# Attention, a top-2 mixture and a top-1 mixture on one core: where the softmax sums, the one-hot products and the first lo parts are computed

## The chip, the core and the metric

The program runs on one NeuronCore of a Trainium2 chip. The metric is the time in device microseconds (us) of one execution. TensorE multiplies matrices into PSUM, VectorE and ScalarE do elementwise work, GpSimd does elementwise work and issues the indirect DMAs, and SyncE issues most other DMAs. In the profile they are PE, DVE, ACT, POOL and SP.

## The reference, cut to what matters

Three stages follow each other. All arithmetic is float32.

```python
# attention: q, k, v are [4, 8, 576, 64]
scores = scale * q @ k^T, masked to blocks of 64: block_i >= block_j
attn = exp(scores - max); attn = attn / (sum(attn) + 1e-9)
x = (attn @ v) as [2304, 512]
# first mixture: 8 experts, the best 2 of each row
noisy = x @ w_gate + log1p(exp(x @ w_noise)) * noise
weights = softmax over the two best; out = sum of weight * (relu(x @ w1[e]) @ w2[e])
# second mixture, on the first one's output: 8 experts, the best 1 of each row
logits = x @ w_gate2 + bias[modality]; e = argmax
out = softmax(logits)[e] * (relu(x @ w1[e]) @ w2[e])
```

## The kernel before

**Precision.** Products that need float32 are made from pairs of a reduced type: a tensor is copied into a hi part by ScalarE, and a lo part, the tensor less its hi part, is computed by another engine. Three matrix products (hi by hi, hi by lo, lo by hi) then stand for one. For a tile of weights this is `Stage.split` (line 450): `act.activation` makes `hi` (in the profile `wh`), `eng.tensor_sub` makes `lo` (`wl`), 128 x 1024 elements at a time. The caller chooses `eng`.

**Attention** goes in 16 pairs of heads (`pair(p)`, line 849), each cut into named steps: scores `S`, maxima `M` (VectorE), exponentials `E` (ScalarE, which also sum up into `ss`), transposes `B` with hi and lo copies `H` and `L` (`PTh`, `PTl`), products with the values `V`, projections `X`, copies `XC`. `R` (line 971) adds the two sums of the last block, `R1` (974) adds 1e-9 to nine sums, `R2` (977) takes reciprocals into `rr`; all three run on VectorE. On GpSimd, `VS` splits the values (`vs`) and `out_rows` (1067) scales a pair's rows by `rr` into `x` and its logits into `LH`.

**The order** of the attention stage is made by a planner at build time (lines 1201 to 1348). Every step has a due time (`SCHED`, line 19, plus 14.5 us per pair) and a list of steps before it (`before`). `clk` holds a modelled time for each engine, from cost formulas (lines 80 to 99). At each turn the planner emits the step of TensorE, ScalarE or VectorE that can start first, among equals the one due first. GpSimd's work is put out along with other steps. What the planner emits is the fixed order of each engine's queue.

**The first routing** (`route`, line 643) is a chain of small VectorE operations on up to 10 columns of 128 rows: logits `lg`, two one-hot choices `oh` (by `onehot`), a mask `m`, counts on TensorE, positions, then for each batch of 576 rows `hot_b` (`sl_ob`, 128 x 1280), `hot_a` (`sl_oa`, 128 x 400, and the product `sl_ov`, 128 x 2000) and `lists`, ten matrix products of the two. It runs for two batches after pair 7, one after pair 11 and one after pair 15 (`route_at`, line 1294); its steps are slipped in between the attention steps. The first two of these calls (`slow` true, three products in all) compute `sl_ov` on GpSimd, and `made` (line 282) tells `lists` when the planner takes it to be done; the last call computes it on VectorE. The last one ends with `ids1`, the rows of every expert (`last_route`, line 1122).

**The jobs** of the mixtures are passes of one expert over a set of rows: `mm1` (first layer, evicted into `kp` or `hh` by ScalarE and `kp` or `hl` by VectorE), then `mm2` (second layer). Job `j00` starts early: its four first-layer weight tiles are loaded into `xs` (called `pre`) and split on GpSimd at planned times (line 1305), and its steps `JT` to `JV` with the splits `JS0` to `JS3` (line 1178: `JS0` and `JS1` on GpSimd, `JS2` and `JS3` on VectorE, tiles `kld` and `qld` of 512 columns each) end the attention stage. The other jobs go through `run` (line 1366): for the first mixture with `ea` and `eb` as `[gps]` (line 1531), so GpSimd makes every lo part, and for the second with VectorE, or VectorE and GpSimd in turn. SyncE loads up to four tiles of weights ahead into `raw`; a buffer is free when its hi and lo parts are made. GpSimd also issues the gathers of rows (`xr`), the scatters of results (`X`) and of logits (`LG`).

## Time and profile before

| | us |
|---|---|
| median of 3 runs (lowest, highest) | 1046.46 (1046.31, 1047.7) |
| the profiled execution, its own time | 1041.64 |
| span of the profiled execution | 1039.6 |
| busy: TensorE matmul, VectorE, ScalarE, GpSimd | 987.5, 741.4, 518.9, 534.2 |
| chain that ended last, share of the span | PE 49%, issue 4%, POOL 3%, DVE 2% |

The profiled execution is one execution; its time is its span and some 2 us around it. Attention takes about the first 300 us, the first mixture runs to about 760, the second to the end. All helpers record line 71, so instructions are told apart by the tiles they write and read (`out<-in`).

### The profile page before, as it was taken

To read this page: it belongs to the slowest core of one execution; us is meant where nothing else is said; L and a number is where in the kernel's file an instruction comes from. 1 tells how busy PE (TensorE), PEld (TensorE's weight loads), DVE (VectorE), ACT (ScalarE), POOL (GpSimd) and SP (SyncE) were. 2 spreads that over 40 slices of the span, in tenths; PEclk is the share of its full clock that TensorE was granted. 3 is DMA by queue.
4 is the path that set the end of the run, shared out by engine and by line. 5 is a ranking of instruction groups with operands and counts; after the bars stand their busy time and mean duration, and the time that the engine had idled before them with its cause. 6 is when DMAs were issued, how large, how long until landed. Compare 5 with 4: busy or idle time off the path is not lost.

```text
span 1039.6 us, 17514 instructions
## 1 busy us (share of the span) xinstructions
PE 987.5 (95%) x6090; PEld 879.0 (85%) x6090; DVE 741.4 (71%) x1766; ACT 518.9 (50%) x1156; POOL 534.2 (51%) x420
## 2 busy tenths in 40 slices
PE   7999998997998799999999999999999999999996
PEld 6888887776787789898989899898978888999995
DVE  6778779888868689647768493948798885554551
ACT  5887876766654225333333333333324545555651
POOL 6123142272346558977668584847658345333231
PEclk8999998998999899999999999999999999999999
DMA  5465433321117455655545372735167767677630
GB/s 127 110 189 163 147 97 96 89 60 39 54 55 212 163 122 132 182 144 134 111 125 120 104 142 81 158 87 102 16 179 204 259 187 253 217 224 225 205 103 13
DMA packets 155954, 141.08 MB, mean 136 GB/s; under 512 B 73929, under 2 KB 122441, under 8 KB 155730
## 3 DMA queue, kind: packets, MB, share of 16 engines
q1 hardware_dynamic: 137794, 106.65, 34.2%
q0 software_dynamic: 18064, 33.23, 15.8%
q8 instruction: 51, 0.84, 0.3%
q14 instruction: 45, 0.37, 0.1%
HBM read 112.01 MB, written 28.36 MB: 135 GB/s over the span
## 4 chain that ended last, share of the span: by engine, by line
PE 49%; issue 4%; POOL 3%; DVE 2%; DMA 1%; ACT 0%; POOLq 0%; SPq 0%
PE ph L71 25%; PE py L71 22%; PE px L71 2%; POOL wl L71 2%; DMA xr<-X,ids 1%; DVE wl L71 1%; POOL LG L71 0%; DMA raw<-in_moe_w_dram 0%; POOL X L71 0%; DMA lgx<-LG 0%; PE pt L71 0%; DVE g_l L71 0%; POOL out_dram L71 0%; DVE g_t L71 0%; DVE kp L71 0%
## 5 line engine op out<-in xcount | busy, mean ns | idle before, releaser
L71 POOL TENSOR_TENSOR wl<-raw,wh 128x1024 fp32r<-128x1024 f32 x88 | 226.8, 2618 | 120.0 <-ACT wh L71 108.1
L71 PE MATMUL ph<-xth,wh 128*128 128x320 f32 (+2 forms) x800 | 242.1, 303 | 6.5 <-DVE kp L71 6.5
L71 PE MATMUL ph<-xtl,wh 128*128 128x320 f32 (+2 forms) x800 | 240.7, 301 | 0.0
L71 PE MATMUL ph<-xth,wl 128*128 128x320 f32 (+2 forms) x800 | 240.6, 301 | 0.0
L71 DVE SCALAR_TENSOR_TENSOR zero<-py,gts,wgb 128x512 f32<-128x512 f32 x304 | 227.5, 748 | 8.2
L71 PE MATMUL py<-wh,kp 128*128 128x512 f32 x496 | 167.9, 399 | 0.0
L71 PEld LDWEIGHTS ph<-xth,wh 128*128 128x128 f32 x800 | 152.4, 190 | 8.2 <-DVE kp L71 7.5
L71 PEld LDWEIGHTS ph<-xtl,wh 128*128 128x128 f32 x800 | 152.5, 191 | 0.7
L71 PEld LDWEIGHTS ph<-xth,wl 128*128 128x128 f32 x800 | 152.4, 190 | 0.0
L71 ACT ACTIVATE wh<-raw 128x1024 fp32r<-128x1024 f32 x144 | 150.9, 1053 | 0.6 <-DMA raw<-in_moe_w_dram 0.4
L71 ACT ACTIVATE yr<-py,gts 128x512 f32<-128x512 f32 x60 | 41.4, 690 | 147.7 <-PE py L71 104.9
L71 PEld LDWEIGHTS py<-wh,kp 128*128 128x128 f32 x496 | 93.9, 189 | 18.7
L71 DVE SCALAR_TENSOR_TENSOR hl<-ph,hh 128x320 fp32r<-128x320 f32 (+2 forms) x100 | 46.4, 466 | 76.3 <-ACT hh L71 76.3
L71 PE MATMUL ps<-kh,kp 128*128 128x256 f32 (+5 forms) x320 | 98.4, 349 | 2.2 <-ACT kp L71 1.0
L71 PE MATMUL py<-wl,kp 128*128 128x512 f32 x248 | 97.2, 392 | 0.0
L71 PE MATMUL py<-wh,hh 128*128 128x512 f32 x232 | 93.9, 405 | 0.0
L71 DVE TENSOR_TENSOR xtl<-px,xth 128x512 fp32r<-128x512 f32 x58 | 40.0, 690 | 74.3 <-ACT xth L71 68.2
L71 PE MATMUL py<-wl,hh 128*128 128x512 f32 x232 | 90.6, 390 | 1.3 <-POOL wl L71 1.3
L71 PE MATMUL py<-wh,hl 128*128 128x512 f32 x232 | 90.8, 391 | 0.0
L71 ACT ACTIVATE p<-ps,nm 128x288 f32<-128x288 f32 (+8 forms) x160 | 79.1, 500 | 22.4 <-DVE nm L71 20.8
L71 DVE TENSOR_TENSOR wl<-raw,wh 128x1024 fp32r<-128x1024 f32 x56 | 70.0, 1259 | 27.8 <-ACT wh L71 27.4
L71 ACT ACTIVATE hh<-ph 128x320 fp32r<-128x320 f32 (+2 forms) x100 | 41.9, 419 | 94.4 <-PE ph L71 91.2
(250 smaller groups left out, 1886.5 us busy)
## 6 DMA issues: line engine op xcount, KB each, us to landing
raw<-in_moe_w_dram SPq DMA_DIRECT2D x144, 512.0 KB
X<-zero SPq DMA_DIRECT2D x13, 512.0 KB
kld<-in_k_dram SPq DMA_DIRECT2D x32, 128.0 KB
qld<-in_q_dram SPq DMA_DIRECT2D x32, 128.0 KB
vld<-in_v_dram SPq DMA_DIRECT2D x32, 128.0 KB
X<-x SPq DMA_DIRECT2D x16, 256.0 KB
xs<-in_moe_w_dram SPq DMA_DIRECT2D x4, 512.0 KB
wgb<-WG2T POOLq DMA_DIRECT2D x1, 2048.0 KB
```

The costliest lines, as they stand in the source:

```text
L71: return f(*a, **kw)
```

## The change

The two sums `R` and `R1` become one step `R` on GpSimd, emitted as soon as a pair's last exponential is. `hot_a` computes its product on VectorE always, in two pieces where it is large; the parameter `slow` and `made` go. The splits of `xs`, of `JS0` and `JS1`, and those of `run` that are emitted before `ids1` use VectorE; the pieces from `xs` are cut to 512 columns.

```diff
--- before.py
+++ after.py
@@ -279,21 +279,22 @@
             yield 1.6
             return ob
 
-        made = [0]
-
-        def hot_a(pool, a, n, a0, na, vals, eng):
+        def hot_a(pool, a, n, a0, na, vals):
 
             oa = pool.tile([128, n, na], BF16, name="sl_oa")
             ov = pool.tile([128, n, NV, na], BF16, name="sl_ov")
             vec.tensor_tensor(oa, bc(lane[:, None, a0:a0 + na], [128, n, na]), bc(a[:, :, None], [128, n, na]), op=OP.is_equal)
             yield .8
-            eng.tensor_tensor(ov, bc(oa[:, :, None, :], [128, n, NV, na]), bc(vals[:, :, :, None], [128, n, NV, na]), op=OP.mult)
-            made[0] = clk["pool"] if eng is gps else 0
-            yield .3
+            m = -(-n // 2) if n * na > 200 else n
+            for c in range(0, n, m):
+                s = slice(c, min(c + m, n))
+                vec.tensor_tensor(ov[:, s], bc(oa[:, s, None, :], [128, s.stop - c, NV, na]),
+                                  bc(vals[:, s, :, None], [128, s.stop - c, NV, na]), op=OP.mult)
+                yield .3
             return ov
 
         def lists(pl, ob, ov, n, first=True, last=True):
-            yield "pe", made[0]
+            yield "pe", 0
             for i in range(n):
                 ten.matmul(pl.rearrange("p v a -> p (v a)"), ob[:, i], ov[:, i].rearrange("p v a -> p (v a)"),
                                  start=(first and i == 0), stop=(last and i == n - 1))
@@ -455,7 +456,11 @@
                 m = 1024 // len(parts)
                 for x, raw in enumerate(parts):
                     act.activation(hi[:, m * x:m * x + m], raw, AF.Copy)
-                    eng.tensor_sub(lo[:, m * x:m * x + m], raw, hi[:, m * x:m * x + m].bitcast(F32))
+
+                    k = 512 if parts[0] is pre else m
+                    for c in range(0, m, k):
+                        d = slice(m * x + c, m * x + c + k)
+                        eng.tensor_sub(lo[:, d], raw[:, c:c + k], hi[:, d].bitcast(F32))
                 (j.wa if w == "a" else j.wb).append([t.rearrange("p (n c) -> p n c", n=4 if w == "a" else 2) for t in (hi, lo)])
 
         class Job:
@@ -640,7 +645,7 @@
         stage = Stage([j00, j10] + firsts + seconds)
 
 
-        def route(b0, nb, slow):
+        def route(b0, nb):
 
             C = 5 * nb
             bs = slice(5 * b0, 5 * (b0 + nb))
@@ -743,7 +748,7 @@
             for b in range(nb):
                 n = slice(10 * b, 10 * b + 10)
                 ob = yield from hot_b(rt, bl[:, n], 10)
-                ov = yield from hot_a(rt, a[:, n], 10, 0, NA1, va[:, n], gps if slow else vec)
+                ov = yield from hot_a(rt, a[:, n], 10, 0, NA1, va[:, n])
                 yield from lists(pl, ob, ov, 10, b == 0, b == nb - 1)
             if b0 == 0:
                 vec.tensor_copy(acc1, pl)
@@ -969,10 +974,8 @@
                         ex(st["s", 8][a], 288 * a, 8, 8 + a)
 
                 def R():
-                    vec.tensor_add(st["ss"][:, 8:9], st["ss"][:, 8:9], st["ss"][:, 9:10])
-
-                def R1():
-                    vec.tensor_scalar(st["ss"][:, 0:9], st["ss"][:, 0:9], 1e-9, None, op0=OP.add)
+                    gps.tensor_add(st["ss"][:, 8:9], st["ss"][:, 8:9], st["ss"][:, 9:10])
+                    gps.tensor_scalar(st["ss"][:, 0:9], st["ss"][:, 0:9], 1e-9, None, op0=OP.add)
 
                 def R2():
                     ss = st["ss"]
@@ -985,7 +988,7 @@
                     two(i)
                 for i in range(4, 8):
                     one(i)
-                f.update(S8=S8, M8=M8, N8=N8, E8=E8, R=R, R1=R1, R2=R2)
+                f.update(S8=S8, M8=M8, N8=N8, E8=E8, R=R, R2=R2)
 
 
                 blocks = [(n, i, j) for j, n0 in ((0, 0), (1, 9), (2, 16), (3, 22)) for n, i in enumerate(range(2 * j, 9), n0)]
@@ -1120,7 +1123,7 @@
                     flags.add("early")
 
             def last_route():
-                yield from route(B - 1, 1, False)
+                yield from route(B - 1, 1)
                 yield from slot_ids(rt, acc1, NA1, 64, pad1.rearrange("p e t -> p (e t)"), ids1, gts1)
                 flags.add("ids1")
                 for t in range(j11.nt):
@@ -1129,7 +1132,7 @@
 
             def routes(i):
                 if i < 2:
-                    yield from route((B - 2) * i, B - 2 - i, True)
+                    yield from route((B - 2) * i, B - 2 - i)
                     yield from early(i)
                 else:
                     yield from last_route()
@@ -1176,7 +1179,7 @@
                     hid_(m)
 
                 def S_(i):
-                    stage.split(vec if i in (2, 3) else gps)
+                    stage.split(vec)
                     fetch_b(1)
                 for i in range(NQ):
                     f["JS%d" % i] = lambda i=i: S_(i)
@@ -1199,23 +1202,25 @@
 
 
             TT, OFF = SCHED[0], dict(SCHED[1])
-            OFF.update(N8=OFF["M8"] + .1, R1=OFF["R"] + .1, R2=OFF["R"] + .2)
+            OFF.update(N8=OFF["M8"] + .1, R2=OFF.pop("R"))
             kinds = dict(T="pe", M="pe", H="act", R="act", S="act", L="dve", V="dve")
 
             def engine(n):
+                if n in ("R", "VS"):
+                    return "pool"
                 if n[0] == "J":
                     return kinds[n[1]]
                 if n[0] in "TSBV" or n in ("X0", "X1"):
                     return "pe"
                 return "act" if n[0] in "HCE" or n in ("QH", "KH", "A4", "XC0", "XC1") else "dve"
 
-            lag = {"pe": .26, "act": .15, "dve": .13}
+            lag = {"pe": .26, "act": .15, "dve": .13, "pool": .3}
             blk = (0, 2, 4, 5, 6, 7, 8)
             S_, E_ = ["S%d" % i for i in blk], ["E%d" % i for i in blk]
             B_, L_ = ["B%d" % m for m in range(6)] + ["BT"], ["L%d" % m for m in range(6)] + ["LT"]
             before = {"TQ": [], "TK": [], "T4": ["TK"], "QH": ["TQ"], "QL": ["QH"], "KH": ["TK"], "KL": ["KH"], "A4": ["T4"], "D4": ["A4"],
-                      "R": E_, "BT": ["E8"], "HT": ["BT"], "LT": ["HT"], "VX": ["L0", "VS"], "CX": ["VX"], "V0": L_ + ["VS"], "V1": L_ + ["VS"],
-                      "C0": ["V0", "CX"], "C1": ["V1", "CX"], "X0": ["C0"], "X1": ["C1"], "XC0": ["X0", "R2"], "XC1": ["X1", "R2"], "R1": ["R"], "R2": ["R1"]}
+                      "BT": ["E8"], "HT": ["BT"], "LT": ["HT"], "VX": ["L0", "VS"], "CX": ["VX"], "V0": L_ + ["VS"], "V1": L_ + ["VS"],
+                      "C0": ["V0", "CX"], "C1": ["V1", "CX"], "X0": ["C0"], "X1": ["C1"], "XC0": ["X0", "R2"], "XC1": ["X1", "R2"], "R2": ["R"]}
             for i in blk:
                 before.update({"S%d" % i: ["QL", "KL"] + ["D4"] * (i == 8), "M%d" % i: ["S%d" % i], "E%d" % i: ["M%d" % i]})
             before.update({"N8": ["M8"], "E8": ["N8"]})
@@ -1257,7 +1262,9 @@
                     steps[p] = pair(p) if p < NPAIR else first_steps()
                 clk["base"] = t
                 steps[p][n]()
-                fin[p, n] = clk["pool" if n == "VS" else engine(n)]
+                fin[p, n] = clk[engine(n)]
+                if n in E_ and all((p, x) in fin for x in E_):
+                    emit(p, "R", t)
                 if n in ("V0", "V1", "VX") and all((p, x) in fin for x in ("V0", "V1", "VX")) and p + 2 < NPAIR:
                     emit(p + 2, "VS", t)
                 if n == "VS" and p + 2 < NPAIR:
@@ -1278,7 +1285,7 @@
                     if p >= k:
                         if (p - k, d) not in fin:
                             return None
-                        t = max(t, fin[p - k, d] + (.3 if d == "VS" else 0 if d[0] in "FG" else lag[engine(d)]))
+                        t = max(t, fin[p - k, d] + (0 if d[0] in "FG" else lag[engine(d)]))
                 if n[0] in bank and e == "pe":
                     b = bank[n[0]][0]
                     m = 2 if n == "S8" else 1
@@ -1302,7 +1309,7 @@
                 at(60 + 10 * i, lambda a=a: blank(*a))
             for i in range(NQ):
                 at(110 + 14 * i, lambda: stage.fetch(1))
-                at(110 + 14 * i + 11, lambda: stage.split(gps))
+                at(110 + 14 * i + 11, lambda: stage.split(vec))
             while any(todo.values()) or len(aside) > 1 or "early" not in flags:
                 best = None
                 for e, l in todo.items():
@@ -1377,7 +1384,7 @@
                 for f in range(len(j.hh), NF // 128):
                     j.mm1(f, hp_)
                     if f in fs and len(j.wb) < NQ:
-                        stage.split(eb[fs.index(f) % len(eb)])
+                        stage.split(eb[fs.index(f) % len(eb)] if "ids1" in flags else vec)
                     stage.fetch(ah)
                     rows()
                     filler()
@@ -1399,7 +1406,7 @@
                                 if left[2]:
                                     break
                                 until(nx.need[0])
-                            stage.split(ea[left[1] % len(ea)])
+                            stage.split(ea[left[1] % len(ea)] if "ids1" in flags else vec)
                             left[1] += 1
                     stage.fetch(ah)
                     filler()
@@ -1517,7 +1524,7 @@
                 for i in range(2):
                     n = slice(HN * i, HN * i + HN)
                     ob = yield from hot_b(pool, bl[:, n], HN)
-                    ov = yield from hot_a(pool, a[:, n], HN, a0, na, vals2[:, n], vec)
+                    ov = yield from hot_a(pool, a[:, n], HN, a0, na, vals2[:, n])
                     yield from lists(pl, ob, ov, HN, i == 0, i == 1)
                 acc = pool.tile([128, NV, na], F32, name="g_acc")
                 vec.tensor_copy(acc, pl)
@@ -1563,7 +1570,7 @@
                 for i in range(B):
                     n = slice(10 * i, 10 * i + 10)
                     ob = done(hot_b(r1, bl[:, n], 10))
-                    ov = done(hot_a(r1, a[:, n], 10, 0, NT2, vals.rearrange("p c k v -> p (c k) v")[:, n], vec))
+                    ov = done(hot_a(r1, a[:, n], 10, 0, NT2, vals.rearrange("p c k v -> p (c k) v")[:, n]))
                     done(lists(pl, ob, ov, 10, i == 0, i == B - 1))
                 acc = r1.tile([128, NV, NT2], F32, name="acco")
                 vec.tensor_copy(acc, pl)
```

## Rows read from the trace of the kernel before

**Rows 1.** Stages: length, busy PE, PEld, DVE, ACT, POOL, granted clock, DMA.
```profile
20.00:150.00 130.00, 128.40 (x860) 112.51 (x860) 101.54 (x250) 103.25 (x329) 29.92 (x46) 0.99 0.52 142
...
150.00:300.00 150.00, 133.36 (x876) 113.96 (x876) 127.09 (x333) 101.76 (x311) 56.14 (x57) 0.95 0.24 65
...
300.00:362.00 62.00, 52.73 (x303) 47.27 (x303) 44.90 (x86) 23.17 (x44) 38.07 (x29) 0.92 0.53 159
...
442.00:760.00 318.00, 318.00 (x1865) 291.55 (x1864) 220.43 (x573) 115.77 (x191) 214.84 (x121) 1.00 0.49 112
```

**Rows 2.** Timeline of TensorE, the five long gaps: start, length; in brackets idle before, releaser.
```profile
173.03 2.82 PE L71 MATMUL pt<-ident,p 128*128 128x128 f32 x12 [4.16 <-DVE PTl L71]
...
238.46 1.12 PE L71 MATMUL pt<-ident,p 128*128 128x128 f32 x4 [5.47 <-DVE PTl L71]
...
274.00 0.63 PE L71 MATMUL pt<-ident,p 128*128 128x128 f32 x4 [2.58 <-DVE oh L71]
...
326.83 0.18 PE L71 MATMUL pt<-m,tri 128*128 128x40 bf16 x1 [3.79 <-DVE m L71]
...
342.94 0.69 PE L71 MATMUL ph<-xth,wh 128*128 128x384 f32 x1 [3.96 <-DVE kp L71]
```

**Rows 3.** Stretches of half clock behind four gaps, and around 274; columns as rows 1.
```profile
173.00:177.80 4.80, 4.77 (x23) 4.68 (x24) 4.80 (x15) 2.65 (x8) 0.00 (x0) 0.51 0.26 90
...
238.50:242.60 4.10, 4.10 (x20) 4.10 (x21) 2.92 (x7) 2.16 (x6) 0.00 (x0) 0.50 0.02 4
...
327.90:331.30 3.40, 3.40 (x12) 2.81 (x10) 1.95 (x5) 1.75 (x3) 0.99 (x1) 0.50 0.46 151
...
343.00:348.40 5.40, 5.40 (x17) 5.40 (x18) 5.24 (x10) 1.15 (x2) 0.00 (x0) 0.50 0.33 98
...
260.00:280.00 20.00, 17.42 (x119) 15.16 (x118) 17.76 (x52) 14.62 (x49) 6.29 (x8) 1.00 0.23 69
```

**Rows 4.** Timeline of VectorE: stretched instructions.
```profile
166.99 1.40 DVE L71 TENSOR_SCALAR ss<-ss 128x9 f32<-128x9 f32 x1
...
168.30 2.87 DVE L71 TENSOR_TENSOR ex<-ex,u 128x80 f32<-128x80 f32 x1
...
231.67 4.96 DVE L71 TENSOR_SCALAR ss<-ss 128x9 f32<-128x9 f32 x1
...
319.63 2.32 DVE L71 TENSOR_TENSOR oh<-oh,e_rev 128x40 f32<-128x40 f32 x1
...
324.61 2.17 DVE L71 TENSOR_TENSOR m<-oh 128x40 bf16<-128x40 f32 x1
...
334.54 7.89 DVE L71 TENSOR_SCALAR d<-e 128x5 f32<-128x5 f32 x1
```

**Rows 5.** Timeline of GpSimd at three of these places.
```profile
168.73 2.34 POOL L71 TENSOR_TENSOR wl<-xs,wh 128x1024 fp32r<-128x1024 f32 x1
...
233.06 3.53 POOL L71 TENSOR_TENSOR sl_ov<-sl_oa,vals 128x2000 bf16<-128x2000 bf16 x1
...
334.80 7.60 POOL L71 TENSOR_TENSOR wl<-raw,wh 128x1024 fp32r<-128x1024 f32 x3
```

**Rows 6.** Groups of VectorE, 150 to 300 us: busy us, mean ns.
```profile
L71 DVE TENSOR_SCALAR ss<-ss 128x9 f32<-128x9 f32 x8 | 13.2, 1648 | 0.9 <-ACT p L71 0.9
...
L71 DVE TENSOR_TENSOR ss<-ss 128x1 f32<-128x1 f32 x7 | 1.1, 156 | 0.2 <-ACT p L71 0.2
```

**Rows 7.** Groups of GpSimd, 0 to 362 us.
```profile
L71 POOL TENSOR_TENSOR wl<-raw,wh 128x1024 fp32r<-128x1024 f32 x8 | 19.6, 2604 | 16.0 <-ACT wh L71 16.0
...
L71 POOL TENSOR_SCALAR mn<-midf 128x18 f32<-128x18 f32 x1 | 0.2, 218 | 0.1
```

**Rows 8.** Groups of VectorE, 300 to 362 us; the last line from the whole profile.
```profile
L71 DVE TENSOR_TENSOR sl_ov<-sl_oa,vals 128x2000 bf16<-128x2000 bf16 x1 | 2.2, 2236 | 0.0
...
L71 DVE TENSOR_TENSOR wl<-kld,wh 128x512 fp32r<-128x512 f32 x2 | 1.4, 681 | 0.0
...
L71 DVE TENSOR_TENSOR wl<-raw,wh 128x1024 fp32r<-128x1024 f32 x56 | 70.0, 1259 | 27.8 <-ACT wh L71 27.4
```

## The prediction

> **What bounds the kernel now.** I read the stages first, then TensorE's gaps, then what VectorE and GpSimd did in them. By stage [rows 1], TensorE works 318.00 of 318 us from 442 to 760, so whatever is won earlier is carried straight through that stage. From 20 to 150 it works 128.40 of 130. The loss lies between: 150 to 300 holds 133.36 us of work in 150, and 300 to 362 holds 52.73 in 62. The timeline of TensorE puts 20.0 us of that into five gaps [rows 2]: 4.16, 5.47, 2.58, 3.79 and 3.96 us. Each ends on a VectorE instruction. Four of them cost twice: the granted clock stands at about 0.5 (1.2 of 2.4 GHz) when TensorE comes back [rows 3], and the 4.77, 4.10, 3.40 and 5.40 us that it then works would have taken half, so 2.4 + 2.05 + 1.7 + 2.7 = 8.8 us are lost. The 2.58 us gap at 274 left the clock at 1.00 (last of rows 3).
>
> Why is VectorE late? Look at durations, not order [rows 4]. `ss`, a sum over 9 columns, takes 1.40 and 4.96 us; `ex`, 80 columns, 2.87; `oh` and `m`, 40 columns, 2.32 and 2.17; `d`, 5 columns, 7.89. Lay GpSimd beside them [rows 5]: its lo part of weights ends at 168.73 + 2.34 = 171.07 and `ex` at 171.17; its one-hot product at 233.06 + 3.53 = 236.59 and `ss` at 236.63; its three lo parts at 334.80 + 7.60 = 342.40 and `d` at 342.43. VectorE stands until GpSimd's last instruction in a row is through; it does not get in between two of them. This is the price that the change goes after.
>
> The Trainium skill (SBUF — State Buffer, Who interferes with whom) gives a reason: a VectorE instruction with two SBUF inputs, or in a mode using both ports, and a GpSimd instruction that reads SBUF exclude each other, and the later one waits in full. The endings above agree.
>
> **The parts and their prices.**
>
> *Sums on GpSimd.* Sixteen pairs lose two VectorE instructions each. Between 150 and 300 the eight adds of 1e-9 take 13.2 us; seven adds of one column take 0.156 each [rows 6]. At that price eight would take 1.3, so 11.9 us of standing go. On GpSimd the two ops cost some 0.2 us each (its 18-column op takes 0.2 [rows 7]), 0.4 per pair. They wait there for the last exponential, and the next pair's values and the scaled rows queue behind them; `R2` waits for them on VectorE. The cover is the schedule: `R2` is due at +9.0 us, the last exponential at -1.75 us, ten us of slack. I charge nothing; if the cover went, `R2` and all VectorE work behind it would be late by at most one GpSimd run, some 3.5 us as the product above. Between 20 and 150 at most 1.6 us can be won [rows 1]; I take 0.
>
> *The lo parts of the first jobs.* Four from `xs` go to VectorE in halves: a 512-column piece there takes 0.681 us [rows 8], so 1.4 each, 5.4 in all. Two of the four in the first job's steps (`JS0`, `JS1`) follow, 2.7 us, in a stretch where TensorE has no gap: nothing. Eight from `raw` before `ids1` [rows 7] at 1.259 each [rows 8] are 10.1 us. No DMA is added; a raw buffer is freed after 1.26 instead of 2.6 us, so SyncE's loads can only start earlier.
>
> *The one-hot products.* Three go from GpSimd (3.53 us) to VectorE, 2.236 us whole [rows 8]; cut in two it pays a second start, 0.10 us by two pieces of 0.681 against one of 1.259, so 2.3 each, 7.0 in all. The fourth was there already and is only cut. `lists` on TensorE no longer waits for GpSimd.
>
> So VectorE gets 5.4 + 2.7 + 10.1 + 7.0 = 25.2 us of new work. What counts is each gap:
> - 173 us: `ss` and `ex` give back 1.24 + 2.7; the lo part adds 1.4. Gain 2.5, and 2.4 of clock, since a gap of 1.7 is left, shorter than the harmless 2.58.
> - 238 us: `ss` gives back 4.8, the product costs 2.3. Gain 2.5, gap left 3.0. This lies between the 2.58 after which the clock held and the 3.79 after which it fell, nearer to the first: I book the 2.05.
> - 274 us: GpSimd's own work (values, scaled rows) stays and still holds the routing's operations; only the share of `ss` goes, about 11.9 / 8 = 1.5.
> - 327 us: `oh` and `m` give back 4.2 (each over the 0.156 of one column), two lo parts add 2.5. Gain 1.7, and 1.7 of clock.
> - 343 us: `d` gives back 7.7, three lo parts add 3.8. That would close the gap; but VectorE is then nearly full there (eight evictions, six lo parts and the last routing within the second job's first layer), so I take 3.0 of the 3.96, and 2.7 of clock.
>
> Sum: 2.5 + 2.4 + 2.5 + 2.05 + 1.5 + 1.7 + 1.7 + 3.0 + 2.7 = 20.0 us.
>
> Against it stands one unknown: the fourteen new pieces between 150 and 300 (eight from `xs`, six of products) also read two SBUF tiles. No row shows such a piece held. Below: 0, if they fall between GpSimd's runs. Above: held as `ss` is, 1.5 each, 21 us. GpSimd's work there falls from 56.14 us [rows 1] by 4 x 2.34 and 3 x 3.53 to 36 of 150, 24%; 14 x 0.24 x 1.5 = 5 us, of which I put 3 on the path. **Sum: 17 us.** The profiled execution took 1041.6 us (span 1039.6 and 2.0 around it), 4.8 under the median of the runs, 1046.5. I take the difference off the median: **1029.5 us**.
>
> **The rivals.**
>
> *The standing only changes its victim.* If every second one of the fourteen pieces is held like `ss`, that is 7 x 1.5 = 10.5 us, and the 2.5 + 2.4 + 2.5 + 2.05 + 1.5 = 11 us won between 150 and 300 are gone. Only the stretch after 300, where little but DMA issues stays on GpSimd, gives its 1.7 + 1.7 + 3.0 + 2.7 = 9.1: about 1037.5 us. (With all fourteen held, 21 us, nothing is won at all.) For it: the pieces meet the same GpSimd work as `ss`. Against: they lie elsewhere than `ss`, which is emitted just as GpSimd scales a pair's rows, and they are short. The Trainium skill (SBUF — State Buffer, Who interferes with whom) speaks for it: an instruction with two SBUF inputs waits in full if GpSimd came first. By that rule each of the fourteen that comes second stands; the trace agrees for `ex`, which reads two SBUF tiles.
>
> *VectorE becomes the bound (slower).* It is busy 127.09 of 150 and 44.90 of 62 us [rows 1], standing included. Its queue is in order: a lo part ahead of an eviction holds the PSUM bank that TensorE needs next. If all 25.2 us of new work reach TensorE, five gaps of 20.0 us become 25.2, and the clock falls as before: 1046.5 + 5 = 1051.5 us. It decides from the point where TensorE's waits for VectorE between 150 and 362 exceed 20 us. Against it: 11.9 us of `ss`, 2.7 of `ex`, 4.2 and 7.7 after 300, 26 us of standing, leave the same queue.
>
> *All gaps close.* The five gaps and the clock: 20.0 + 8.8 = 28.8, 1017.7 us. Against: the gap at 274 is made by work that stays.
>
> *A new order eats it.* The planner builds another order of the attention steps from the changed costs, and the second routing's gates are placed by the same clock. The gain moves a few us either way, or is lost: 1046 us.
>
> **How the numbers follow.** Forecast 0.60 (own range 1022 to 1037), standing moved 0.16, all gaps close 0.10, slower 0.09, lost in the order 0.05. The range 1018 to 1043 leaves out the slower case, the lost one and the tip of the full one. A difference of 0.2% (2 us) is about what a measurement of this kernel can tell from none. Faster: 0.60 + 0.15 + 0.10 = 0.85; slower 0.10; the same 0.05.
>
> **What would show it.** `ss` gone from VectorE; none of its small operations over 2 us between 150 and 360; lo parts of 0.68 and 1.26 us on VectorE there; TensorE's gaps before its solid stage under 10 us in sum; at most one stretch at 0.5 of the clock after 150; the solid stage beginning some 17 us earlier and as long as before. I am wrong if gaps as large end on VectorE's lo parts or products, if these pieces last far longer than 0.7 to 1.3 us, or if the stage after 760 grows by what was won.

## The result, and the profile after

The changed kernel takes **1028.93 us** (median of 4 runs, 1028.7 to 1030.77) against 1046.38 us for the kernel before (4 runs beside it, 1044.7 to 1047.7): a ratio of **0.9838, 95% interval 0.982 to 0.9856**. The forecast was 1029.5 us. Its profiled execution took 1028.72 us with a span of 1026.9, close to its median; that of before took 1041.64, which is 4.8 us under its median. So the two traces can account for 12.7 us of span, not for 17.4. The kernel before and the changed one were measured beside each other a second time, at the end of the experiments: there the gain was 10.6 us (1041.09 to 1030.49), and the two intervals do not meet. So the gain is known only as 10.6 to 17.4 us.

The page of the changed kernel, part 1 and two groups of part 5: VectorE is busy 17 us less than before although it got new work, GpSimd 36 us less.

```profile
PE 983.7 (96%) x6090; PEld 875.1 (85%) x6090; DVE 724.0 (71%) x1761; ACT 519.3 (51%) x1156; POOL 498.4 (49%) x433
...
L71 POOL TENSOR_TENSOR wl<-raw,wh 128x1024 fp32r<-128x1024 f32 x80 | 207.5, 2623 | 105.3 <-ACT wh L71 91.1
...
L71 DVE TENSOR_TENSOR wl<-raw,wh 128x1024 fp32r<-128x1024 f32 x64 | 79.6, 1252 | 29.7 <-ACT wh L71 29.5
```

Eight lo parts from `raw` have moved: 64 on VectorE where [rows 8] has 56.

Stages of the changed kernel (length, then busy PE, PEld, DVE, ACT, POOL, granted clock, DMA share, GB/s); the last three lines are the stretches of half clock between 150 and 427:

```profile
150.00:300.00 150.00, 138.74 (x922) 118.30 (x922) 130.28 (x347) 103.82 (x316) 45.64 (x67) 0.98 0.28 73
300.00:346.00 46.00, 41.59 (x248) 36.72 (x247) 34.44 (x85) 20.57 (x37) 8.01 (x12) 1.00 0.61 175
...
427.00:746.00 319.00, 319.00 (x1874) 292.74 (x1873) 221.52 (x575) 115.47 (x192) 215.66 (x121) 1.00 0.50 111
...
170.60:174.00 3.40, 3.17 (x15) 3.18 (x16) 3.40 (x13) 1.91 (x6) 0.00 (x0) 0.50 0.81 206
...
211.50:214.90 3.40, 3.40 (x17) 3.31 (x16) 3.40 (x6) 2.75 (x8) 0.00 (x0) 0.50 0.40 112
...
382.20:385.60 3.40, 3.06 (x7) 2.48 (x8) 0.28 (x2) 0.00 (x0) 3.40 (x2) 0.50 0.98 272
```

Against [rows 1], 150 to 300 holds 922 matmuls where it held 876, and its clock is 0.98 for 0.95. The next stretch has its clock at 1.00 (0.92 before). The solid stage is as solid as it was, and as long.

Two milestones place the gain, and serve all the experiments. **A** is the start of the last `ps<-kh,wh`, a product of the first job's steps; there are 32 of them in each kernel, and they end the attention stage. **B** is TensorE's return from the wait for the gathered rows `xr`. A came at 314.1 us before and comes at 307.2: 6.9 us won. B came at 361.3 and comes at 346.0: 15.3 us, 8.4 of them between A and B. The first layer of a later job (the first `ph` of 320 columns) starts at 425.43 (438.28 before): 12.85 us, so 2.5 were given back. Here and in the table below, differences are taken between rounded times.

The timeline of TensorE in the changed kernel (start, length; in brackets the idle time before and who ended it):

```profile
170.82 1.97 PE L71 MATMUL pt<-ident,p 128*128 128x128 f32 x8 [2.23 <-DVE PTl L71]
...
190.45 0.66 PE L71 MATMUL pt<-ident,p 128*128 128x128 f32 x4 [1.26 <-DVE PTl L71]
...
210.63 0.66 PE L71 MATMUL pt<-ident,p 128*128 128x128 f32 x4 [3.33 <-DVE PTl L71]
...
249.39 0.77 PE L71 MATMUL pt<-ident,p 128*128 128x128 f32 x5 [1.16 <-DVE PTl L71]
...
267.07 0.63 PE L71 MATMUL pt<-ident,p 128*128 128x128 f32 x4 [0.56 <-DVE pos L71]
...
319.15 0.18 PE L71 MATMUL pt<-m,tri 128*128 128x40 bf16 x1 [1.09 <-DVE m L71]
...
332.43 0.45 PE L71 MATMUL ph<-xth,wh 128*128 128x384 f32 x1 [0.39 <-DVE kp L71]
...
346.00 0.66 PE L71 MATMUL px<-ident,xr 128*128 128x128 f32 x4 [2.87 <-DMA xr<-X,ids]
...
382.54 0.80 PE L71 MATMUL py<-wh,kp 128*128 128x512 f32 x1 [3.86 <-DVE zero L71]
```

Of the five gaps of [rows 2], 20.0 us in sum, the first is 2.23 us now. The 5.47 us stood at the second batch's product of the first routing; in the changed kernel that product runs at 228 to 232 us, and no gap of 0.5 us or more lies between 219 and 249. Where the second routing begins, 1.16 and 0.56 stand for 2.58, and after A 1.09 and 0.39 for 3.79 and 3.96. A gap of 3.33 at 210 is new. Two waits took some back: `xr` now costs 2.87 us (1.45 before), and a bank held by `zero`, the product of the logits on VectorE, costs 3.86 us at 382, which before did not cost anything.

VectorE at 150 to 300 in the changed kernel, timeline:

```profile
150.10 1.71 DVE L71 TENSOR_TENSOR wl<-xs,wh 128x512 fp32r<-128x512 f32 x2 [2.03 <-ACT wh L71]
...
167.24 2.25 DVE L71 TENSOR_TENSOR wl<-xs,wh 128x512 fp32r<-128x512 f32 x2 [0.57 <-ACT wh L71]
...
186.25 3.43 DVE L71 TENSOR_TENSOR wl<-xs,wh 128x512 fp32r<-128x512 f32 x2 [1.65 <-ACT wh L71]
...
205.03 1.71 DVE L71 TENSOR_TENSOR wl<-xs,wh 128x512 fp32r<-128x512 f32 x2 [1.02 <-ACT wh L71]
206.67 3.12 DVE L71 TENSOR_TENSOR g<-e,g 128x10 f32<-128x10 f32 x1
```

Its groups there (busy us, mean ns, idle before):

```profile
L71 DVE TENSOR_TENSOR wl<-xs,wh 128x512 fp32r<-128x512 f32 x8 | 9.1, 1178 | 5.3 <-ACT wh L71 5.3
...
L71 DVE TENSOR_TENSOR sl_ov<-sl_oa,vals 128x1000 bf16<-128x1000 bf16 x6 | 7.1, 1186 | 0.0
```

And GpSimd beside `g`, timeline:

```profile
206.86 1.68 POOL L71 TENSOR_TENSOR vs<-vld,vs 128x512 fp32r<-128x512 f32 x2
208.51 1.25 POOL L71 TENSOR_TENSOR x<-xu,rr 128x640 f32<-128x640 f32 x1
209.73 0.45 POOL L71 TENSOR_TENSOR LH<-xu,rr 128x160 f32<-128x160 f32 x1
```

This reads as [rows 4, 5] did, with one difference. The lo pieces are held (9.1 us for eight, where 0.681 each would be 5.4), and `g`, 10 columns, stands 3.12 us until GpSimd's `x` ends at 208.51 + 1.25 = 209.76; `g` ends at 209.79. But GpSimd's row goes on with `LH` at 209.73, and `g` did not wait for it: "it does not get in between two of them" holds for the rows that the prediction read, not for every row. What is new is 5.3 us in four waits in which VectorE stood with a lo part from `xs` at the head of its queue and ScalarE's hi part not yet made. The gap of 3.33 us at 210 follows directly on such a wait, two lo pieces and `g`.

### The profile page after: what moved, and what is told of

Read it like the earlier page. It is cut to its first block, busy times and chain, and to the rows that moved or that the text cites. A ratio compares the mean times of both kernels' runs of the same rounds, so it can differ in the third digit from the quotient of the medians.

```text
span 1026.9 us, 17498 instructions
## 1 busy us (share of the span) xinstructions
PE 983.7 (96%) x6090; PEld 875.1 (85%) x6090; DVE 724.0 (71%) x1761; ACT 519.3 (51%) x1156; POOL 498.4 (49%) x433
## 4 chain that ended last, share of the span: by engine, by line
PE 78%; DVE 9%; issue 5%; ACT 3%; POOL 2%; DMA 2%; POOLq 0%; SPq 0%; ACTq 0%
PE ph L71 27%; PE py L71 25%; PE pt L71 9%; PE ps L71 7%; PE pa L71 6%; PE px L71 2%; DVE wl L71 2%; DMA xr<-X,ids 1%; POOL wl L71 1%; DVE PTl L71 1%; ACT p L71 1%; ACT wh L71 1%; DVE nm L71 1%; DVE kp L71 1%; POOL LG L71 0%
## 5 line engine op out<-in xcount | busy, mean ns | idle before, releaser
L71 POOL TENSOR_TENSOR wl<-raw,wh 128x1024 fp32r<-128x1024 f32 x80 | 207.5, 2623 | 105.3 <-ACT wh L71 91.1
L71 DVE SCALAR_TENSOR_TENSOR zero<-py,gts,wgb 128x512 f32<-128x512 f32 x296 | 221.6, 749 | 8.2
L71 PEld LDWEIGHTS py<-wh,kp 128*128 128x128 f32 x496 | 93.9, 189 | 22.7 <-DVE zero L71 4.1
L71 DVE TENSOR_TENSOR wl<-raw,wh 128x1024 fp32r<-128x1024 f32 x64 | 79.6, 1252 | 29.7 <-ACT wh L71 29.5
L71 POOL DMA_INDIRECT xr<-X,ids x55 | 57.8, 1051 | 75.2 <-PE px L71 45.1
```

The costliest lines, as they stand in the source:

```text
L71: return f(*a, **kw)
```

## The experiments

Each run has the kernel before beside it on the same chip. Its median there was 1043.46 us (27 runs) for engines alone, order alone, sums back and lo parts back, 1043.28 (14) for the run without the add, products back, the logits read from SBUF and the first run of later lo parts, and 1041.09 (11) for the other four. Ratios are to these. The medians of before differ by up to 5 us from series to series, so runs of different series are compared by their ratios; those of the changed kernel are 0.9838 (0.982 to 0.9856) and 0.9906 (0.9887 to 0.9925). The theory after the result: VectorE instructions of some forms (two SBUF inputs, or a `TENSOR_SCALAR` on SBUF) stand while GpSimd runs; the change takes those holds away, and that is the gain. The rival: the planner made a better order, and the engines matter little.

### Engines or order

**Engines alone.** The planner is charged as before and emits the order of before; only the engine of the instructions changes.

```diff
+    vec_p, gps_v = Timed(nc.vector, "pool", pool_cost), Timed(nc.gpsimd, "dve", dve_cost)
-                    vec.tensor_scalar(st["ss"][:, 0:9], st["ss"][:, 0:9], 1e-9, None, op0=OP.add)
+                    gps_v.tensor_scalar(st["ss"][:, 0:9], st["ss"][:, 0:9], 1e-9, None, op0=OP.add)
-                at(110 + 14 * i + 11, lambda: stage.split(gps))
+                at(110 + 14 * i + 11, lambda: stage.split(vec_p))
```

(not shown: the other moved instructions, likewise; products and lo parts stay in one piece, as before)

> The kernel before, whose planner is charged as before, so that every queue of TensorE, ScalarE and VectorE keeps its order; only the engine of the sums, of the first lo parts and of the three products is the changed one. Theory (GpSimd's runs hold VectorE up): the five gaps shrink although the order is the old one, 1031 to 1037 us. Rival (the planner's new order makes the gain): 1044 to 1049 us.

Measured: 1051.61 us, ratio **1.0087 (1.0059 to 1.0115)**, slower. The theory as it stood falls, and the rival's range is passed too. Its stage, its waits of VectorE and of TensorE from 150 to 305 us (sum in us, number, longest), then the last of these waits in the kernel before, and VectorE's timeline at one of them:

```profile
150.00:300.00 150.00, 125.68 (x788) 108.03 (x788) 114.91 (x296) 94.81 (x288) 42.64 (x62) 0.91 0.23 63
```

```profile
DVE wl L71 <- ACT wh L71: 6.9, 4, 2.4
...
DVE rr L71 <- POOL ss L71: 5.4, 3, 2.7
...
PE pt L71 <- DVE PTl L71: 22.7, 8, 4.5
```

```profile
PE pt L71 <- DVE PTl L71: 13.4, 6, 5.5
```

```profile
149.96 1.23 DVE L71 TENSOR_TENSOR wl<-xs,wh 128x1024 fp32r<-128x1024 f32 x1 [2.02 <-ACT wh L71]
153.90 0.75 DVE L71 RECIPROCAL rr<-ss 64x5 f32<-64x5 f32 x4 [2.71 <-POOL ss L71]
```

In six microseconds VectorE stands 2.02 us for a hi part and 2.71 us for GpSimd's sum, and the evictions `PTl` that TensorE needs are queued behind both. Where `ss` had been held for GpSimd, `rr` now waits for GpSimd. The holds of `ss` are gone, waits in order took their place, and other holds stay (`sl_ov` takes 3.53 us at 245.20, 2.236 alone [rows 8]): A comes at 327.3 us, 13.2 later than before. After A, where only lo parts and the last routing are concerned, the same kernel gains: from A to B it needs 39.8 us, before 47.2, the changed kernel 38.8.

**Order alone.** The reverse: the order of the change, the engines of before (not shown: the products and the lo parts of the jobs, likewise).

```diff
+    vec_p, gps_v = Timed(nc.vector, "pool", pool_cost), Timed(nc.gpsimd, "dve", dve_cost)
-                    gps.tensor_scalar(st["ss"][:, 0:9], st["ss"][:, 0:9], 1e-9, None, op0=OP.add)
+                    vec_p.tensor_scalar(st["ss"][:, 0:9], st["ss"][:, 0:9], 1e-9, None, op0=OP.add)
-                at(110 + 14 * i + 11, lambda: stage.split(vec))
+                at(110 + 14 * i + 11, lambda: stage.split(gps_v))
```

> The changed kernel's order, with the sums, the first lo parts and the three products back on the engines that they had before. Theory (holds): VectorE is held up again by lo parts and products, 1042 to 1052 us, small VectorE operations of 2 us and more again. Rival (order): 1027 to 1032 us.

Measured: 1040.74 us, 0.998 (0.9956 to 1.0003): no change that can be told. Timelines of TensorE, VectorE and GpSimd in it:

```profile
171.57 1.97 PE L71 MATMUL pt<-ident,p 128*128 128x128 f32 x8 [3.88 <-DVE PTl L71]
...
321.00 0.66 PE L71 MATMUL px<-ident,xs 128*128 128x128 f32 x4 [3.52 <-DVE xtl L71]
...
339.53 0.69 PE L71 MATMUL ph<-xth,wh 128*128 128x384 f32 x1 [4.97 <-DVE kp L71]
```

```profile
329.35 6.60 DVE L71 TENSOR_SCALAR sl_a<-sl_a 128x10 f32<-128x10 f32 x1
```

```profile
328.29 7.62 POOL L71 TENSOR_TENSOR wl<-raw,wh 128x1024 fp32r<-128x1024 f32 x3
```

The holds after A are back, as `sl_a` for 6.60 us until three lo parts on GpSimd are through (329.35 + 6.60 = 335.95, 328.29 + 7.62 = 335.91): from A to B 49.1 us. But A comes at 307.8, 6.3 us earlier than before, nearly all that the changed kernel has. Of that 1.2 was there before the first gap began (171.57 - 3.88 = 167.69, before 168.87, changed 168.59). The adds of 1e-9 are still on VectorE, only elsewhere: seven of them between 150 and 300 have a mean of 601 ns, where [rows 6] has 1648. So both fall in part: up to A the new order by itself gives most of what the change has, from A to B only the engine gives anything.

**Engines alone, sums given to GpSimd at once.** If it is the late sum that `rr` waits for, giving it out as soon as the last exponential is emitted, as the change does, should help (not shown: the two sums are in `RS`; `R` and `R1` only charge their planned time).

```diff
                 fin[p, n] = clk["pool" if n == "VS" else engine(n)]
+                if n in E_ and all((p, x) in fin for x in E_):
+                    steps[p]["RS"]()
```

> The engines-only kernel (old order of TensorE, ScalarE and VectorE, changed engines) with one difference: GpSimd gets the sums as soon as a pair's last exponential is emitted, as in the changed kernel, and not at the old place of the steps. Theory (the loss of the engines-only kernel is 5.4 us of VectorE waiting for sums that stood behind values on GpSimd, and lo parts put in without slack): 1042 to 1047 us, VectorE's wait for the sums mostly gone. Rival (it is the lo parts and products alone): 1049 to 1053 us.

Measured: 1054.88 us, 1.0125 (1.01 to 1.015). The theory was wrong. VectorE's wait for the sums there, beside the same 6.9 us for hi parts:

```profile
DVE rr L71 <- POOL ss L974: 4.9, 3, 2.7
```

The wait of `rr` is 4.9 us instead of 5.4: on GpSimd the sum still stands behind the split of the values `vs`. What the change has and this kernel lacks is a place for `R2` that is computed from GpSimd's modelled time, later in VectorE's queue; in the changed kernel no wait of VectorE for `ss` appears, and `rr` starts 2 to 10 us behind its sum. Which of the unplanned pieces (`R2`, lo parts, products) costs most of the 8 to 14 us was not separated.

### What each part gives

The first of these runs keeps the order of before. In the others the planner charges the engine that is used and makes an order of its own, so engine and order change together.

**Only the held instruction taken away.** Before, in its own order, without the add of 1e-9, whose time the planner still charges.

```diff
-                    vec.tensor_scalar(st["ss"][:, 0:9], st["ss"][:, 0:9], 1e-9, None, op0=OP.add)
+                    clk["dve"] = max(clk["dve"], clk["base"]) + dve_cost("tensor_scalar", st["ss"][:, 0:9], None, {})
```

> The kernel before without the add of 1e-9 to the sums (left out; the sums are 1 or more), the planner charged as if it were there, so that the order of all queues is the old one. It takes 16 VectorE instructions away and adds nothing. Theory (standing of ss is on the path): 11.9 us of standing between 150 and 300 go, the gaps at 173, 238 and 274 us shrink by 1.2, 4.8 and 1.5 and one half-clock stretch goes: 6 to 10 us under the kernel before. Rival (the next two-input operation in VectorE's queue is held in its place): within 2 us of the kernel before.

Measured: 1035.16 us, **0.9909 (0.988 to 0.9938)**, 8.1 us less, within the expected 6 to 10. TensorE's timeline where [rows 2] has 5.47 us, and the stage:

```profile
230.00 0.66 PE L71 MATMUL pt<-ident,p 128*128 128x128 f32 x4 [0.59 <-DVE PTl L71]
```

```profile
150.00:300.00 150.00, 141.04 (x958) 121.77 (x957) 119.80 (x335) 105.03 (x320) 61.41 (x59) 0.98 0.26 70
```

A comes 12.0 us earlier, at 302.1; from A to B it is 47.6 us, as before. The 12.0 are too much: this execution took 1029.43 us, the fastest of the five, and it was 2.2 us ahead before the gap at 173 began. By the medians sixteen adds on nine columns give 8 us, in the order of before. By its columns such an instruction is worth a fraction of a microsecond; its price is the hold [rows 6].

**Sums back on VectorE**, all else as changed (`R` and `R1` on `vec` as two planned steps):

```diff
-                    gps.tensor_scalar(st["ss"][:, 0:9], st["ss"][:, 0:9], 1e-9, None, op0=OP.add)
+                    vec.tensor_scalar(st["ss"][:, 0:9], st["ss"][:, 0:9], 1e-9, None, op0=OP.add)
-                if n in ("R", "VS"):
+                if n == "VS":
```

> The changed kernel with the two sum steps on VectorE again, planned as before. Theory (holds, and the long ones come from lo parts and products): only the holds by scaled rows and values return, about 1.2 us a pair, part of it on the path: 1030 to 1035 us. Rival (the sums are the larger part of the gain): 1038 us or more.

Measured: 1036.77 us, 0.994 (0.9914 to 0.9965). The ratio is 0.3 to 1.0% above those of the changed kernel, 4 to 11 us; the lower end is not clear of noise. The time lies between the two expectations, nearer the rival's. A comes at 312.4, 5.2 later than in the changed kernel. So giving up the sums' move seems to cost something once VectorE has the lo parts too; whether by holds or by the other order was not separated.

**Lo parts back on GpSimd**, all that the change moved (not shown: those from `xs` are in one piece):

```diff
-                    stage.split(vec)
+                    stage.split(vec if i in (2, 3) else gps)
-                at(110 + 14 * i + 11, lambda: stage.split(vec))
+                at(110 + 14 * i + 11, lambda: stage.split(gps))
-                        stage.split(eb[fs.index(f) % len(eb)] if "ids1" in flags else vec)
+                        stage.split(eb[fs.index(f) % len(eb)])
-                            stage.split(ea[left[1] % len(ea)] if "ids1" in flags else vec)
+                            stage.split(ea[left[1] % len(ea)])
```

> The changed kernel with all first lo parts (from xs, in the first job's steps, and in the jobs before the last routing's end) on GpSimd again. Theory: the gaps at 173, 327 and 343 us and their half clock return, 14 us by the prediction's terms: 1040 to 1045 us. Rival (VectorE gains as much from the lost work as it loses by holds): 1029 to 1034 us.

Measured: 1032.39 us, 0.9893 (0.986 to 0.9926): the rival's number. TensorE:

```profile
316.41 0.18 PE L71 MATMUL pt<-m,tri 128*128 128x40 bf16 x1 [0.67 <-DVE m L71]
...
331.54 0.69 PE L71 MATMUL ph<-xth,wh 128*128 128x384 f32 x1 [5.34 <-DVE kp L71]
```

The gap of `kp` returns, 5.34 us, as expected, and from A to B it is 44.0 us instead of 38.8. That of `m` does not return, A comes at 306.1, 1.1 us earlier than in the changed kernel, and the 3.86 us wait for `zero` at 382 is gone. So 5.2 us are lost between A and B and part of it is won elsewhere. The ratio lies between the two of the changed kernel: what the lo parts are worth as a whole cannot be told from nothing.

**Products back on GpSimd** in the first two calls of `route`:

```diff
-                ov = yield from hot_a(rt, a[:, n], 10, 0, NA1, va[:, n])
+                ov = yield from hot_a(rt, a[:, n], 10, 0, NA1, va[:, n], gps if b0 + nb < B else vec)
```

> The changed kernel with the first two routings' three products on GpSimd again, whole, as before. Theory: with ss gone from VectorE nothing stands behind each product but the routing's own operations: 1029 to 1034 us. Rival (the product on GpSimd was the cause of the 238 us gap whatever stands behind it): 1034 to 1038 us, with a gap of 4 us or more before the second batch's lists.

Measured: 1031.75 us, 0.9876 (0.9842 to 0.9909), in the theory's range and, by its ratio, not to be told from the changed kernel. A comes at 310.7.

**Uncut pieces.** The lo parts from `xs` and the products whole:

```diff
-            m = -(-n // 2) if n * na > 200 else n
+            m = n
-                    k = 512 if parts[0] is pre else m
+                    k = m
```

> The changed kernel with the lo parts from xs and the products on VectorE in one piece each (128 x 1024 and 128 x 2000). Theory of the prediction (a second start costs 0.10 us, and the pieces may fall between GpSimd's runs): within 2 us of the changed kernel. Rival (short pieces let evictions and GpSimd in between): 1033 us or more, with a longest TensorE gap over 4 us between 150 and 300.

Measured: 1027.93 us, 0.9875 (0.9853 to 0.9897), beside 1030.49 for the changed kernel in the same series. A and B come at 308.1 and 344.8. The rival's 1033 us are not reached, and TensorE's longest gap between 150 and 300 is 2.46 us here. That the pieces are short gives nothing that can be measured.

### The hold by itself

The 3.86 us at 382 come from a row of `zero` instructions that read PSUM (`py`) and hold its banks. They can read the copy `yr` in SBUF instead, which frees the banks sooner. This run lets them do so while eight or more of them wait:

```diff
-    direct = "places" in flags
+    direct = "places" in flags and len(fill) < E
```

> The changed kernel, in which the logits of a result tile are summed from its SBUF copy instead of from PSUM while eight or more such sums wait. It aims at the wait that took the place of those removed: 3.9 us of TensorE behind VectorE's zero at 382 us and the half clock after it. Theory (that wait is a held PSUM bank): the wait goes, 1022 to 1026 us. Rival (VectorE is simply full there and another wait comes): 1027 to 1030 us.

Measured: 1043.01 us, 0.9994 (0.9976 to 1.0012): 12 us or more worse than the changed kernel, and both expectations wrong. One input has moved from PSUM to SBUF; VectorE's queue keeps its order there. `zero` by its tile (duration ns least, median, most), first here, then in the changed kernel, there in both forms:

```profile
L71 DVE SCALAR_TENSOR_TENSOR zero<-yr,wgb x64: 673/691/5933, 352.9 to 809.6; 128x512 f32<-128x512 f32 x64
```

```profile
L71 DVE SCALAR_TENSOR_TENSOR zero<-yr,wgb x24: 680/691/694, 352.7 to 373.8; 128x512 f32<-128x512 f32 x24
...
L71 DVE SCALAR_TENSOR_TENSOR zero<-py,gts,wgb x296: 737/751/753, 374.6 to 796.3; 128x512 f32<-128x512 f32 x148
```

Timelines of VectorE, GpSimd and TensorE here:

```profile
389.14 3.75 DVE L71 SCALAR_TENSOR_TENSOR zero<-yr,wgb 128x512 f32<-128x512 f32 x1
...
393.67 5.93 DVE L71 SCALAR_TENSOR_TENSOR zero<-yr,wgb 128x512 f32<-128x512 f32 x1
```

```profile
389.39 2.94 POOL L71 TENSOR_TENSOR wl<-raw,wh 128x1024 fp32r<-128x1024 f32 x1
...
393.83 5.22 POOL L71 TENSOR_TENSOR wl<-raw,wh 128x1024 fp32r<-128x1024 f32 x2
```

```profile
400.87 0.69 PE L71 MATMUL ph<-xth,wh 128*128 128x384 f32 x1 [5.12 <-DVE kp L71]
```

`zero` with two SBUF tiles does its 0.6 us of work when GpSimd's lo parts have ended: 393.83 + 5.22 = 399.05, and 399.60 is its end. In the changed kernel the form that reads `py` takes 753 ns at most in 296 instructions (mean 749), beside the same GpSimd work. The wait for the bank went as expected; a gap of 5.12 us and smaller ones (2.91 and 2.15 the longest) came. This is the cleanest control of the hold. The Trainium skill (SBUF — State Buffer, Who interferes with whom) says that a VectorE instruction with at most one SBUF input, outside the modes that use both ports, does not contend with GpSimd; the trace agrees, 0.75 against up to 5.93 us.

### What is left in the changed kernel

The 5.3 us that VectorE stands for the hi parts of `xs` (the expectation's 7.5 is too much: 2.03 + 0.57 + 1.65 + 1.02 = 5.27) should go if the lo parts are given out 2 us later in planned time:

```diff
-                at(110 + 14 * i + 11, lambda: stage.split(vec))
+                at(110 + 14 * i + 11, lambda i=i: stage.split(vec, lambda f: at(110 + 14 * i + 11 + 2, f)))
```

(`split` hands its lo parts to that second argument)

> The changed kernel with the four lo parts from xs emitted 2 us of planned time after their hi parts. In the changed kernel VectorE stands idle for 7.5 us in front of them, waiting for ScalarE's hi part, and they take 9.1 us for 5.4 us of work. Theory (these are costs of the place in the queue): the idle time goes, the gaps at 171, 190 and 211 us shrink: 1022 to 1027 us. Rival (the planner's new order takes as much): 1028 to 1032 us.

Measured: 1026.05 us, 0.9817 (0.9781 to 0.9853), in the theory's range. Two of the four lo parts in VectorE's timeline, and the stage:

```profile
168.80 1.22 DVE L71 TENSOR_TENSOR wl<-xs,wh 128x512 fp32r<-128x512 f32 x2
184.02 1.29 DVE L71 TENSOR_TENSOR wl<-xs,wh 128x512 fp32r<-128x512 f32 x2 [0.23 <-ACT wh L71]
```

```profile
150.00:300.00 150.00, 140.99 (x956) 119.14 (x956) 128.29 (x350) 105.07 (x321) 44.38 (x68) 1.00 0.28 76
```

The 0.23 us is all that is left of the 5.3, and three of the four pairs aren't held either. TensorE gets 956 matmuls done there instead of 922, at a clock of 1.00; the gaps at 171 and 207 are 1.53 and 1.09 us. One of 2.45 us at 264, behind the routing's `sl_a`, is new, and VectorE's later wait for the hi part of the first `kld` grows from 2.28 to 5.17 us. A comes at 303.1, 11.0 us before that of the kernel before. Both kernels again, side by side:

> The kernel with the lo parts from xs 2 us of planned time after their hi parts, beside the changed kernel on the same chip. Theory (the place in the queue is worth it): 2 to 5 us under the changed kernel, its ratio to the kernel before 0.979 to 0.983. Rival (chance of the chip): no difference.

> The changed kernel again, to stand beside the others of this chip. All theories: ratio to the kernel before 0.982 to 0.987.

Measured: 1026.58 us, 0.9873 (0.9844 to 0.9903), and the changed kernel 1030.49 us, 0.9906 (0.9887 to 0.9925). The difference of 3.9 us is in the expected 2 to 5; both expected ratios were missed, mainly because the kernel before was faster here (1041.09 us). The later lo parts by their tile in this second run, and those of the changed kernel in its first:

```profile
L71 DVE TENSOR_TENSOR wl<-xs,wh x8: 628/688/1162, 148.7 to 198.9; 128x512 fp32r<-128x512 f32 x8
```

```profile
L71 DVE TENSOR_TENSOR wl<-xs,wh x8: 692/1074/2458, 150.1 to 205.6; 128x512 fp32r<-128x512 f32 x8
```

Most of the pieces are no longer held, a median of 688 ns against 1074. Whether the waits or the holds had cost more was not separated. It has the lowest median of the versions, by 3.9 us in the one series that has both, but the intervals overlap. Behind B most of the lead is lost again: 6.9 us at B (338.4 against 345.3) are 2.7 us of span (1025.1 against 1027.8). In that series the change gains 0.9%, in the first measurement 1.6%: the kernel before has medians of 1041.09 to 1046.38 us over four series, the changed one 1028.93 and 1030.49 over two.

The two milestones over the runs, in us, each from one trace:

| kernel | A | A to B | B |
|---|---|---|---|
| before | 314.1 | 47.2 | 361.3 |
| changed (two runs) | 307.2; 306.5 | 38.8; 38.8 | 346.0; 345.3 |
| engines alone; with early sums | 327.3; 329.6 | 39.8; 42.2 | 367.1; 371.8 |
| order alone | 307.8 | 49.1 | 356.9 |
| before without the add | 302.1 | 47.6 | 349.7 |
| changed, sums back; products back | 312.4; 310.7 | 38.0; 38.0 | 350.4; 348.7 |
| changed, lo parts back | 306.1 | 44.0 | 350.1 |
| changed, pieces uncut | 308.1 | 36.7 | 344.8 |
| changed, lo parts later (two runs) | 303.1; 300.4 | 38.0; 38.0 | 341.1; 338.4 |

From A to B every kernel with the lo parts on VectorE needs 36.7 to 42.2 us, every one with them on GpSimd 44.0 to 49.1, in either order. In each of the latter four one operation on ten columns or fewer stands there for 6.60 to 8.10 us; in the others the longest VectorE instruction is a whole product, 2.24 us. That is shown. A says less: the two runs with later lo parts are the same kernel and differ by 2.7 us at A, all of it there when their first gap begins, at 169.0 and 166.2 us; the clock over the first 20 us was 0.91 in the one, 1.00 in the other. Up to A order and holds both count, and how the 6.9 us divide between them was not separated: order alone has 6.3, the add left out of the old order more than 6.9, the engines alone lose 13.2.

## Why the prediction was right

**The number.** 1029.5 forecast, 1028.93 measured. The sum behind it was 17 us, and the traces show 12.7; the two measurements show 17.4 and 10.6. It was taken off the median of before; taken off the profiled execution, 1041.6, it would have given 1024.6, some 4 us too low. The 4.8 us by which that execution was quick cover the difference, so that the forecast time came out to within 0.6 us is in part luck. Why executions of before differ is not to be seen in one trace.

**From A to B.** 1.7 + 1.7 + 3.0 + 2.7 = 9.1 us were booked, 8.4 came. The gaps fell from 3.79 to 1.09 and from 3.96 to 0.39, more than booked; the clock came whole (no half clock is left there); 1.4 went to `xr`. These make 9.3, so 0.9 is not placed. Right, in size and cause.

**Up to A.** 11.0 less 3 were booked, 6.9 came: right in size, and only in part for the reason given. The gaps named shrank: by 1.9 where 2.5 was booked, the 5.47 us went whole where 2.5 was booked, and 0.9 for 1.5. But the order-alone run has 6.3 of the 6.9 with the sums still on VectorE, so the size came in part by luck. The rival of a new order, given 0.05 and priced as a gain eaten up, was at work here as a gain. In the order of before the standing itself was worth what the prediction said, 8 us of median for the add alone. Two steps failed. First, "a gap of 1.7 is left, shorter than the harmless 2.58": 2.23 was left, and a new gap of 3.33 came at 210. Second, 2.4 + 2.05 of clock were booked as won. TensorE still works 3.17 and 3.40 us at half clock, which loses 1.6 + 1.7 = 3.3 us, so 4.45 - 3.3 = 1.1 came. What both lacked is a wait without a price in the sum: the lo part at the head of VectorE's queue waits for ScalarE's hi part, 5.3 us in four waits, and the evictions stand behind it. With the lo parts given out 2 us later A comes 11.0 us early, the clock holds at 1.00, and the waits and most of the holds of the pieces from `xs` are gone; that order is a new one too.

**Sums on GpSimd at nothing**, because "the cover is the schedule": right in the changed kernel, where no wait of VectorE for `ss` shows and the ops cost 0.19 and 0.25 us. The price named "if the cover went" was tried in effect by the engines-alone run: 2.7 us at a time, 5.4 in three waits.

**The fourteen pieces held.** 5 us charged; the eight from `xs` were held for 9.1 - 5.4 = 3.7 us, and the products were not: 1.186 us a piece, 2.4 a pair where 2.3 was priced. The size is near; of what went into it, GpSimd's work there was 45.64 us, not 36.

**Behind B.** "The solid stage beginning some 17 us earlier": 12.85. The sum had no term for what the earlier start meets: the 3.86 us at `zero`, with half clock behind it (0.50 over 382.2 to 385.6). On balance 2.5 us were given back.

**The rivals.** The standing did change its victim in part: the lo pieces stood 3.7 us and `g` 3.0, 6.7 of the 10.5 that this rival priced. The slower kernel did not come about in the change. In the engines-alone run it did: TensorE's waits for `PTl` from 150 to 305 alone are 22.7 us (13.4 before), past the 20 at which that rival decides, and the run is 8 us slower than its before, where the rival had 5. But VectorE is not full there, it is busy 114.91 us of 150, 127.09 before; it stands in order, with the evictions behind it.

**The signs named.** `ss` left VectorE, the solid stage is as long as before, and the stage behind it did not take back what was won (1026.9 - 746 = 280.9 us, before 279.6). The others failed: `g` took 3.12 us where no small operation was to pass 2; two pieces from `xs` at 186 us took 3.43 us together; three stretches of half clock are left before the solid stage, where at most one was named; and the gaps shown above are 16.8 us in sum where under 10 was named. The forecast holds, its picture of the stage from 150 to 300 only in part.

## What to carry to other kernels

When a tiny VectorE instruction takes microseconds, look at what GpSimd runs at that moment: removing or moving it is worth the hold, not its columns, and one operand in PSUM can be the cure. When an instruction moves to another engine in a queue of fixed order, plan its place anew, behind what it waits for: moved without that, the same change made this kernel slower. A sum of gains belongs against the execution it was read from, so know where that one stands among its runs.

## What the runs showed of the hardware that was not expected

- A hold can outlast one GpSimd instruction: `zero`, 0.69 us of work, took 5.93 beside two lo parts in a row, and `sl_a`, a `TENSOR_SCALAR` on ten columns, 6.60 beside three. It need not last a whole row: `g` was done at 209.79, 0.06 us after GpSimd's next instruction had begun.
- The same instruction with one operand in PSUM, beside the same GpSimd work, was not held: 0.753 us at most in 296.
- The clock stood at 0.50 behind a TensorE gap of 2.23 us (170.6 to 174.0), while the 2.58 us gap in [rows 2] left it at 1.00, and so did one of 2.45 us with the later lo parts. So the length of the last gap alone does not tell whether the clock falls.
